# Other places in the issue order for one chunk's tokens, two weight pieces and the root steps of a fused mLSTM and Fourier kernel

## The chip, the cores and the metric

The kernel runs on one core of a Trainium2 chip. The metric is device time of one execution in microseconds, the median of several runs. The kernel before takes 398.78 us (three runs, 398.45 to 399.27).

A core has a matrix engine (TensorE, PE in the profile, with PEld for its weight loads), VectorE (DVE), ScalarE (ACT), GpSimd (POOL) and SyncE (SP), which here only issues DMA transfers. Each works off a queue of its own in order; semaphores hold an instruction until what it reads has been written and what it overwrites has been read.

## The reference

```python
batch, n_heads, seq, head_dim = (4, 8, 768, 40)
for t in range(S):                                   # mLSTM cell
    m_new = np.maximum(f_gate[:, :, t] + m, i_gate[:, :, t])
    f_stab = np.exp(f_gate[:, :, t] + m - m_new)
    i_stab = np.exp(i_gate[:, :, t] - m_new)
    m = m_new
    C = f_stab[:, :, None, None] * C + i_stab[:, :, None, None] * np.einsum('bhd,bhe->bhde', vt, kt)
    n = f_stab[:, :, None] * n + i_stab[:, :, None] * kt
    h_tilde = np.einsum('bhde,bhe->bhd', C, qt)
    denom = np.maximum(np.abs(np.einsum('bhd,bhd->bh', n, qt)[:, :, None]), 1.0)
    y[:, :, t] = h_tilde / denom / (1.0 + np.exp(-o_gate[:, :, t]))
x = y.transpose(0, 2, 1, 3).reshape(B, S, H * D)     # (4, 768, 320)
mixed = np.real(np.fft.fft(np.fft.fft(x, axis=1), axis=2))
u = x + mixed
un = (u - mean(u)) / np.sqrt(var(u) + 1e-06)         # over the last axis
out = u + np.maximum(un @ w_ch1, 0.0) @ w_ch2        # w_ch1 (320, 1280), w_ch2 (1280, 320)
```

## The kernel before

**Order by hand.** Every step is a function entered into a plan with `at(slot, phase, fn, ...)`; the plan is run in order of slot and then of phase (EVAC 0, FILL 1, MAIN 2, FILL_PE 3, with fractions between). Steps thus become instructions in that order, and each instruction goes to the queue of its engine. A step's place in the plan decides only what stands ahead of it on the engines that it uses.

**The mLSTM.** Tokens are processed in 6 chunks of 128 a batch, in a chunked form: scores of queries and keys, weighted by exponentials of gates (`mlstm_exp`, L548), a state C carried from chunk to chunk, and a division by the denominator. Batch 0 goes through `plan_mlstm`, three slots a chunk; the other batches go through `plan_halves`, in halves of 64 tokens, interleaved with the MLP of the batch before. For one chunk of batch 0: `mlstm_from_state` and `mlstm_from_chunk` make the heads (PE, `hb<-qg,C` and `hb<-W,kvt`), `mlstm_to_state` the chunk's part of the state (`pc`), `mlstm_add` (L643) adds it to C on VectorE, `mlstm_decay` (L586) scales C on GpSimd. `mlstm_heads` copies the heads out of PSUM (L630), `mlstm_turn` (L636) transposes them into `px`, a PSUM tile with a single buffer, and `mlstm_finish` (L759 to L766) reads `px`: denominator `den` (L759 to L761), output gate `so` (L763), then the product that writes the chunk's rows of `x` (L766).

**Rows at the wrong end.** For the Fourier step, chunks 3, 4 and 0 run backwards in time in a layout where one token of chunk 4 belongs into row 0 of chunk 3, and chunk 3's own row 0 into row 0 of chunk 4 (likewise chunks 1 and 0). `mlstm_rows` moves these: part 0 saves chunk 3's row (ScalarE, L773, `s_last`), part 1 copies chunk 4's row to chunk 3 (VectorE, L775), part 2 writes the saved row to chunk 4 (ScalarE, L777).

**The Fourier step.** `mix_fold` (L859 to L871) adds and subtracts chunks in pairs (0, 5), (1, 4), (2, 3), the last pair first, into `fe` (and `fe_odd` for the second pair); for batch 0 VectorE makes the sums, GpSimd the differences of the pairs (2, 3) and (1, 4). `mix_seq` (L937) multiplies by the sequence DFT (`pz`), `mix_feat` (L970) by the feature DFT (`pu`). `mix_add` (L984 to L998) adds the result to x chunk by chunk in the order 0, 5, 1, 4, 2, 3 and takes mean and variance; for chunk 4 it first copies one row of its own (L984, L985) that a product of `mix_feat` writes (`hb`). `mix_center` (L1006, ScalarE) subtracts the mean, `mix_turn` (L1017) transposes on TensorE and `mix_turn_out` (L1022, ScalarE) copies the result to `uT`.

**The root.** `mix_rstd` (L1030 to L1035, VectorE) makes a first guess of 1/sqrt(var), and three calls of `mix_rstd_step` (L1041 to L1044, four GpSimd instructions each) refine it. It is used when the MLP's output is scaled and stored (`mlp_store`, L1252).

**The MLP and its weights.** `mlp_in` (L1101, L1110) makes `pm` from `uT`, `mlp_relu` (L1126, ScalarE) the activation `h`, `mlp_out` (L1246) the output. The two weight matrices arrive as 64-bit floats, in ten pieces of 640 KB (five each), and every piece is turned into 32-bit floats on the chip: `load` (L452, a DMA into one of two `raw` buffers), `take` (L462, L464, VectorE: exponent and mantissa bits into `e` and `m`, one buffer each), `convert` (L469, L470, ScalarE) and `join` (VectorE, in three parts: L477 makes `e`, L480 `m`, L484 their product `w_sb`). Pieces are counted from 0 in the code, so the change's pieces 3 and 4 are `pieces[2]` and `pieces[3]`. The list `when` gives the plan's places of take, convert and join.

**Around the change.** VectorE's order from chunk 1's statistics (L998) on is: row copies and addition of chunk 4 (L984 to L998), joining `e` of piece 3, addition of chunk 2 and of chunk 3, joining `m` and `w_sb` of piece 3, taking piece 4. ScalarE's order at that place is: centring of chunks 4 and 2, eight exponentials of batch 1, conversion of piece 4, `uT`, `h`.

Of the kernel before, what the change touches and what calls it, by code (L numbers as in the profile page):

```python
# [10 lines left out]
FP = mybir.dt.float32  # L11
# [8 lines left out]
L = 128  # L20
# [37 lines left out]
def kernel(  # L58
# [379 lines left out]
    class Piece:  # L438
# [26 lines left out]

        def convert(self):
            if self.float:
                return
            nc.scalar.activation(out=self.e, in_=self.e, func=AF.Relu, scale=2.0**23, bias=ebias)  # L469
            nc.scalar.activation(out=self.m.bitcast(FP), in_=self.m, func=AF.Copy, scale=2.0**-20, bias=1.0)  # L470

# [274 lines left out]

    def mlstm_finish(b, c):

        k = chunks.pop((b, c))
        if c == 0:  # L750
            xs[b] = x_bufs[b % 2]
            nc.gpsimd.memset(xs[b][:, :, DM:DM + 1], 0.0)
        h1 = k.px.rearrange("p (a n) (i e) -> p a (n i) e", a=2, i=2) if b == 0 else k.ph
        den = tp.tile([L, H], FP, name="den", tag="den")

        def two(t):
# [7 lines left out]
                                       op0=OP.add, op1=OP.mult)  # L764
        x, sc = (t.rearrange("p (a h d) -> p a h d", a=2, d=D) for t in (xs[b][:, c, 0:DM], k.so))
        nc.vector.tensor_tensor(out=x, in0=h1[:, :, :, 0:D], in1=sc, op=OP.mult)  # L766

# [11 lines left out]
    def plan_mlstm(b):  # L779
        for c in range(NT):  # L780
# [18 lines left out]
            t, phase = ((6, 0.3), (9, -0.3), (12, -0.3), (15, -0.3), (16.5, 0.4), (18.5, 0))[c]  # L799
            at(t, FILL + phase, mlstm_finish, b, c)  # L800
        for c, part, t, phase in ((1, 0, 7, 0.3), (1, 1, 9, -0.2), (1, 2, 10, -0.1), (4, 0, 16, 0.01), (4, 1, 16.5, 0.45),
                                  (4, 2, 18, 0)):
            at(t, FILL + phase, mlstm_rows, b, c, part)

    def plan_halves(b, s0, stride=3):
        at(s0 - 2, FILL + 0.7, halves_start, b)
        for c in range(NT):
# [9 lines left out]
            at(s - 1, FILL, mlstm_scale_v, b, c)  # L817
            e = s - 1 if (b, c) != (1, 0) else s - 2
            at(e, FILL, mlstm_exp, b, c, 0)
            at(e, FILL + 0.5, mlstm_exp, b, c, NP)  # L820
            at(s, FILL, mlstm_mask, b, c)
# [224 lines left out]
    def plan_mix(b, s0, x_done, s_feat, s_add, s_turn):  # L1046
# [31 lines left out]
        for c, a, t in zip(ORDER, s_add, s_turn):  # L1078
            at(a, FILL if b < 2 else MAIN + 0.5, mix_add, b, c)
            at(*((a, FILL + 0.25) if b == 0 and c in (4, 2) else (t, FILL + 0.1)), mix_center, b, c)  # L1080
            at(t, FILL_PE + (5 if b == 0 or c in ORDER[:4] else -0.1), mix_turn, b, c)
            if b > 0:
                at(t, FILL_PE + 6, mix_turn_out, b, c)
            elif t < s_mlp:
                at(t + 1, FILL + 0.2, mix_turn_out, b, c)
            else:
                at(t + 1, EVAC, mix_turn_out, b, c)
# [291 lines left out]
    def plan_batch(b, s_mlstm, s_mix, s_mlp):  # L1379
# [21 lines left out]
        for n in range(3):  # L1401
            at(s + 3 * n if b == 0 else s, FILL + 0.65, mix_rstd_step, b)
        plan_mlp(b, s_mlp)
# [9 lines left out]

    when = [((2, 0.7), (4, 0.5), None), ((18.5, 0.7), (20, 0.7), (21, 0.6)), ((21.5, 0.7), (26, 0.7), None)]
    when += [((s, 0.7), (s + 1, 0.7), (s + 2, 0.6)) for s in (31, 33, 36, 39, 42, 48, 51)]
    pieces = w1_pieces + w2_pieces
    for n, (w, p) in enumerate(zip(when, pieces)):
        if n > 2:
            at(when[n - 2][2][0] + 1 if n != 4 else 31, FILL + 0.7, p.load)
        for t, fn in zip(w, (p.take, p.convert, p.join)):  # L1420
            if t:
                at(t[0], FILL + t[1], fn)
    for part, s in enumerate((7, 10, 13)):
        at(s, FILL - 0.35, pieces[0].join, part)
    for part in range(3):
        at(28 + part, FILL + 0.3, pieces[2].join, part)

# [161 lines left out]
```

## Time and profile before

| what | value |
| --- | --- |
| median of the runs | 398.78 us (398.45 to 399.27) |
| the profiled execution | 400.37 us, of which 398.5 us are its span |
| ScalarE, GpSimd: share of the span | 44%, 34% |
| DMA | 43.96 MB in 21614 packets, mean 110 GB/s |

All times within the trace are microseconds from the start of the span. A timeline row has start, duration, engine, line, operation, `out<-in` by the program's names, shapes and `x` the number of instructions in the row; in brackets at its end stands how long the engine idled ahead of it and which engine's instruction released it. Rows of like instructions are drawn together, and ends of matmuls are modelled, so rows of TensorE can overlap by some tenths.

### The profile page before, as it was taken

How to read it: one execution, taken by the hardware profiler on the slowest of the kernel's cores; microseconds unless marked ns; L12 is line 12 of the kernel's file. 1: busy time of each engine (PE TensorE's matmuls, PEld its weight loads, DVE VectorE, ACT ScalarE, POOL GpSimd, SP SyncE). 2: the span in 40 equal slices, each digit the busy share in tenths (PEclk: the TensorE clock that was granted, in tenths of full speed). 3: DMA queues.
4: the chain of work that ended last, by engine and by line, in shares of the span. 5: the costliest groups of instructions: out<-in, count | busy, mean ns of one | idle time of the engine just before them, and what ended most of it. 6: DMA issues, size and time to landing. Idle time of an engine off the chain costs nothing.

```text
span 398.5 us, 10881 instructions
## 1 busy us (share of the span) xinstructions
PE 383.7 (96%) x4342; PEld 278.1 (70%) x4342; DVE 280.7 (70%) x668; ACT 175.3 (44%) x505; POOL 134.1 (34%) x238
## 2 busy tenths in 40 slices
PE   8999897989999999999999998999999999999996
PEld 6887454545667677656469898766579997556996
DVE  8788859987699466779774688777854785336652
ACT  5978656675433233574442324563440023454000
POOL 5753325674855332363241314562300000020000
PEclk9999899899999999999999999999999999999999
DMA  7968496596983233455000713620000000000000
GB/s 223 305 182 317 107 238 194 159 251 198 258 207 91 89 100 128 137 176 165 2 1 9 231 62 113 194 67 3 0 2 16 19 33 35 0 0 2 34 35 33
DMA packets 21614, 43.96 MB, mean 110 GB/s; under 512 B 3492, under 2 KB 9852, under 8 KB 21436
## 3 DMA queue, kind: packets, MB, share of 16 engines
q1 hardware_dynamic: 21564, 43.27, 36.2%
q8 instruction: 34, 0.56, 0.6%
q14 instruction: 16, 0.13, 0.1%
HBM read 39.16 MB, written 4.10 MB: 109 GB/s over the span
## 4 chain that ended last, share of the span: by engine, by line
PE 78%; DVE 12%; issue 3%; POOL 1%; ACT 1%; DVEq 0%; POOLq 0%; ACTq 0%
PE po L1302 21%; PE pm L1173 16%; PE po L1246 8%; PE pm L1178 6%; PE ph L579 4%; PE pm L1110 4%; PE pu L970 3%; PE ps L579 3%; PE pz L925 2%; DVE so L763 2%; PE pm L1101 2%; PE put L1017 1%; PE hb L579 1%; PE pzt L925 1%; PE pz L937 1%
## 5 line engine op out<-in xcount | busy, mean ns | idle before, releaser
L1252 DVE SCALAR_TENSOR_TENSOR x<-po,rstd,x 128x160 f32<-128x160 f32 (+1 forms) x69 | 27.2, 394 | 39.4 <-PE po L1302 36.3
L1182 DVE TENSOR_TENSOR h<-h,pm 128x384 f32<-128x384 f32 x60 | 30.6, 549 | 26.7 <-PE pm L1178 12.4
L575 POOL TENSOR_SCALAR_AFFINE_SELECT W<-W 64x512 f32<-64x512 f32 x36 | 28.1, 781 | 36.2 <-ACT W L548 32.8
L1173 PE MATMUL pm<-uT,w_sb 128*128 128x384 f32 x90 | 37.8, 507 | 0.2 <-DVE uT L1161 0.2
L702 POOL TENSOR_TENSOR C<-C,decB 128x164 f32<-128x164 f32 x33 | 18.3, 555 | 57.1 <-DVE C L709 55.8
L548 ACT ACTIVATE W<-W,colT 128x64 f32<-128x64 f32 x144 | 36.5, 336 | 0.0
L1110 PE MATMUL pm<-uT,w_sb 128*128 128x384 f32 x80 | 30.6, 514 | 3.7 <-ACT h L1126 1.9
L1246 PE MATMUL po<-w_sb,h 128*128 128x320 f32 x120 | 34.1, 435 | 0.0
L560 POOL TENSOR_TENSOR qg<-qk,Gb 128x512 f32<-128x512 f32 x21 | 28.0, 1335 | 11.6 <-DMA qk<-in_qkT 11.3
L1041 POOL TENSOR_TENSOR t<-rstd 128x6 f32<-128x6 f32 x12 | 4.0, 334 | 81.7 <-DVE v L1035 81.2
L1302 PE MATMUL po<-T,S 128*128 128x160 f32 x180 | 28.0, 302 | 1.1 <-DVE x L1252 1.1
L1246 PEld LDWEIGHTS po<-w_sb,h 128*128 128x128 f32 x120 | 22.3, 190 | 9.2 <-issue 0.6
L1302 PEld LDWEIGHTS po<-T,S 128*128 128x128 f32 x180 | 25.4, 190 | 2.7 <-DVE x L1252 1.3
L1178 PE MATMUL pm<-uT,w_sb 64*128 64x384 f32 x120 | 26.6, 511 | 0.3 <-DVE h L1182 0.3
L1302 PE MATMUL po<-w_sb,h 128*128 128x160 f32 x180 | 26.3, 300 | 0.0
L1302 PEld LDWEIGHTS po<-w_sb,h 128*128 128x128 f32 x180 | 25.2, 190 | 1.5 <-DVE x L1252 0.3
L1173 PEld LDWEIGHTS pm<-uT,w_sb 128*128 128x128 f32 x90 | 15.4, 189 | 13.9 <-DVE h L1182 5.9
L1110 PEld LDWEIGHTS pm<-uT,w_sb 128*128 128x128 f32 x80 | 14.2, 194 | 15.0 <-issue 4.4
L1229 ACT ACTIVATE h<-h 128x384 f32<-128x384 f32 x45 | 23.1, 520 | 3.0 <-DVE h L1182 3.0
L1006 ACT ACTIVATE uc<-x 128x384 f32<-128x384 f32 x24 | 14.4, 614 | 20.7 <-DVE x L998 20.7
L709 DVE TENSOR_TENSOR C<-C,ps 128x164 f32<-128x164 f32 x33 | 10.5, 318 | 16.7 <-PE ps L579 10.0
L1178 PEld LDWEIGHTS pm<-uT,w_sb 64*128 64x128 f32 x120 | 12.9, 185 | 13.0 <-issue 8.2
(259 smaller groups left out, 848.6 us busy)
## 6 DMA issues: line engine op xcount, KB each, us to landing
kvt<-in_kv SPq DMA_DIRECT2D x24, 336.0 KB
qk<-in_qkT SPq DMA_DIRECT2D x48, 160.0 KB
raw<-in_w SPq DMA_DIRECT2D x10, 640.0 KB
Gb<-G_d SPq DMA_DIRECT2D x42, 128.0 KB
W<-M_d SPq DMA_DIRECT2D x36, 128.0 KB
so<-in_o SPq DMA_DIRECT2D x24, 160.0 KB
out<-x SPq DMA_DIRECT2D x24, 160.0 KB
ds_sb<-in_dft_s SPq DMA_DIRECT2D x1, 1158.0 KB
```

Source lines behind the costliest of these rows:

```text
L548: nc.scalar.activation(out=k.W[:, h, :], in_=M, func=AF.Exp, scale=-1.0, bias=colT[:, c, 0, b * H + h:b * H + h + 1])
L560: nc.gpsimd.tensor_tensor(out=k.qg[:, :, t], in0=k.qk[:, 0, :, t], in1=k.Gb[:, :, t], op=OP.mult)
L575: nc.gpsimd.affine_select(out=W, in_=W, compare_op=OP.is_ge, fill=0.0, base=base, pattern=[[0, H], [-1 if back else 1, LH]], channel_multi ...
L579: nc.tensor.matmul(out, w, x, start=start, stop=True, skip_group_check=True)
L1110: nc.tensor.matmul(k.pm[i], w1_block(ch, f // 2 * 2 + i), u[2 * ch], start=(ch == 0 and not ahead), stop=(ch == 1 and ahead), skip_group_c ...
L1173: nc.tensor.matmul(bank, w, u, start=start, stop=True, skip_group_check=True)
L1178: nc.tensor.matmul(bank, w1_rest(i)[rows], mlp_u(gr, 1)[rows], start=False, stop=True, skip_group_check=True)
L1182: nc.vector.tensor_tensor(out=h, in0=h, in1=bank, op=OP.add)
L1229: nc.scalar.activation(out=h, in_=h, func=AF.Relu, scale=-1.0)
L1246: nc.tensor.matmul(k.po[m], hidden(gr, f)[:, i * L:(i + 1) * L], w2_sb[:, f, :], start=(f == 0), stop=(f == NFF - 1))
L1252: nc.vector.scalar_tensor_tensor(out=u, in0=po, scalar=k.rstd[:, c:c + 1], in1=u, op0=OP.mult, op1=OP.add)
L1302: nc.tensor.matmul(po, a[:, f], w[:, f], start=start and f == 0, stop=f == half - 1, skip_group_check=True)
```

## The change

It moves and splits steps; nothing else is computed.

- `mlstm_add` of chunks 1, 2 and 3 stood behind a third of the joining of weight piece 1 (FILL - 0.35); that third now comes at FILL - 0.28, behind the add.
- `mlstm_finish` of chunk 4 has two parts. Part 0 makes `den` and `so` and then the product for one row, which is written directly to row 0 of chunk 3; the copy of that row (`mlstm_rows` part 1) is left out. Part 1 makes the product for all 128 rows; it stands behind the fold of pair (2, 3) and ahead of the fold of pair (1, 4).
- Weight piece 3: its conversion and the joining of `e` come before chunk 0's addition to x; `m` and `w_sb` are joined between chunk 1's statistics and chunk 4's row copies. Piece 4: its taking follows there, its conversion goes in two halves between the centrings of chunks 4 and 2, and its joining stands behind chunk 3's statistics. Its raw load, and that of piece 5, move ahead on SP: the order of issues there was so, raw, so, Gb, Gb, raw and is raw, so, raw, so, Gb, Gb.
- The eight exponentials of batch 1's first chunk are issued as two lots of four with the conversion of piece 4 and a centring between. The centring of chunk 3 moves ahead of one copy of `uT`.
- The root steps of batch 0 go from slots 43, 46 and 49 to 48, 49 and 50. On GpSimd the first now stands behind the last state decay of batch 1 and ahead of the fold into `fe_odd`, the other two behind that fold and ahead of batch 2's first `qg`.

TensorE's order is the same in both kernels.

```diff
-        def convert(self):
+        def convert(self, part=None):
             if self.float:
                 return
-            nc.scalar.activation(out=self.e, in_=self.e, func=AF.Relu, scale=2.0**23, bias=ebias)
-            nc.scalar.activation(out=self.m.bitcast(FP), in_=self.m, func=AF.Copy, scale=2.0**-20, bias=1.0)
+            if part != 1:
+                nc.scalar.activation(out=self.e, in_=self.e, func=AF.Relu, scale=2.0**23, bias=ebias)
+            if part != 0:
+                nc.scalar.activation(out=self.m.bitcast(FP), in_=self.m, func=AF.Copy, scale=2.0**-20, bias=1.0)
...
-    def mlstm_finish(b, c):
-
-        k = chunks.pop((b, c))
+    def mlstm_finish(b, c, part=None):
+
+        k = chunks.pop((b, c)) if part != 0 else chunks[b, c]
...
+        def tokens(rows, to):
+            x, sc = (t.rearrange("p (a h d) -> p a h d", a=2, d=D) for t in (xs[b][rows, to, 0:DM], k.so[rows]))
+            nc.vector.tensor_tensor(out=x, in0=h1[rows, :, :, 0:D], in1=sc, op=OP.mult)
+
+        if part == 1:
+            return tokens(slice(0, L), c)
...
-        x, sc = (t.rearrange("p (a h d) -> p a h d", a=2, d=D) for t in (xs[b][:, c, 0:DM], k.so))
-        nc.vector.tensor_tensor(out=x, in0=h1[:, :, :, 0:D], in1=sc, op=OP.mult)
+        tokens(*((slice(0, 1), c - 1) if part == 0 else (slice(0, L), c)))
...
-            at(t, FILL + phase, mlstm_finish, b, c)
-        for c, part, t, phase in ((1, 0, 7, 0.3), (1, 1, 9, -0.2), (1, 2, 10, -0.1), (4, 0, 16, 0.01), (4, 1, 16.5, 0.45),
+            if c == 4:
+                at(t, FILL + phase, mlstm_finish, b, c, 0)
+                at(17, FILL + 0.15, mlstm_finish, b, c, 1)
+            else:
+                at(t, FILL + phase, mlstm_finish, b, c)
+        for c, part, t, phase in ((1, 0, 7, 0.3), (1, 1, 9, -0.2), (1, 2, 10, -0.1), (4, 0, 16, 0.01),
                                   (4, 2, 18, 0)):
...
-            e = s - 1 if (b, c) != (1, 0) else s - 2
-            at(e, FILL, mlstm_exp, b, c, 0)
-            at(e, FILL + 0.5, mlstm_exp, b, c, NP)
+            early = (b, c) == (1, 0)
+            at(*((27, FILL + 0.22) if early else (s - 1, FILL)), mlstm_exp, b, c, 0)
+            at(*((28, FILL + 0.3) if early else (s - 1, FILL + 0.5)), mlstm_exp, b, c, NP)
...
-            at(*((a, FILL + 0.25) if b == 0 and c in (4, 2) else (t, FILL + 0.1)), mix_center, b, c)
+            at(*(((32, EVAC + 0.1) if c == 3 else (a, FILL + 0.25) if c in (4, 2) else (t, FILL + 0.1)) if b == 0 else
+                 (t, FILL + 0.1)), mix_center, b, c)
...
-            at(s + 3 * n if b == 0 else s, FILL + 0.65, mix_rstd_step, b)
+            at(48 + n if b == 0 else s, FILL + 0.65, mix_rstd_step, b)
...
-    when = [((2, 0.7), (4, 0.5), None), ((18.5, 0.7), (20, 0.7), (21, 0.6)), ((21.5, 0.7), (26, 0.7), None)]
-    when += [((s, 0.7), (s + 1, 0.7), (s + 2, 0.6)) for s in (31, 33, 36, 39, 42, 48, 51)]
+    when = [((2, 0.7), (4, 0.5), None), ((18.5, 0.7), (20, 0.7), (21, 0.6)), ((21.5, 0.7), (23, 0.15), None)]
+    when += [((26, 0.7), None, (29, 0.5)), ((30, 0.7), (34, 0.7), (35, 0.6))]
+    when += [((s, 0.7), (s + 1, 0.7), (s + 2, 0.6)) for s in (36, 39, 42, 48, 51)]
...
-            at(when[n - 2][2][0] + 1 if n != 4 else 31, FILL + 0.7, p.load)
+            at(when[n - 2][2][0] + 1 if n != 4 else 27, FILL + 0.7, p.load)
...
-        at(s, FILL - 0.35, pieces[0].join, part)
-    for part in range(3):
-        at(28 + part, FILL + 0.3, pieces[2].join, part)
+        at(s, FILL - 0.28, pieces[0].join, part)
+    for part, (s, phase) in enumerate(((24, -0.1), (26, 0.3), (26, 0.32))):
+        at(s, FILL + phase, pieces[2].join, part)
+    for part in range(2):
+        at(27, FILL + (0.23, 0.3)[part], pieces[3].convert, part)
```

## The prediction

> **What bounds the kernel now.** I read the page first: its span and the busy shares.
>
> ```profile
> span 398.5 us, 10881 instructions
> PE 383.7 (96%) x4342; PEld 278.1 (70%) x4342; DVE 280.7 (70%) x668; ACT 175.3 (44%) x505; POOL 134.1 (34%) x238
> ```
>
> TensorE is busy for 96% of the span. Only two things can be won back: the 14.8 us in which it stands, and time in which its clock is halved. The profiled execution took 400.37 us, 1.87 us more than its span and 1.59 us more than the median 398.78 of the runs shown; all terms below are taken from its trace, and their sum is applied to the median. The change lies between 30 and 116 us, so the second view was TensorE's waits there, grouped by releaser (total us, times, longest); these lead the list, three shorter ones come below with their own rows.
>
> ```profile
> PE pm L1110 <- ACT h L1126: 1.9, 1, 1.9
> PE pm L1110 <- issue: 1.6, 1, 1.6
> ```
>
> The third view was busy time and granted clock in stretches (TensorE, its weight loads, VectorE, ScalarE, GpSimd; then clock, DMA share, GB/s).
>
> ```profile
> 39.00:42.40 3.40, 2.31 (x17) 1.54 (x16) 3.16 (x7) 2.67 (x10) 2.00 (x3) 1.00 0.15 44
> 42.40:45.80 3.40, 3.40 (x9) 1.13 (x8) 3.12 (x9) 2.28 (x10) 1.88 (x4) 0.51 0.69 193
> 66.30:69.70 3.40, 1.59 (x6) 0.88 (x7) 3.05 (x5) 2.73 (x7) 2.96 (x5) 1.00 0.65 228
> 69.70:73.10 3.40, 3.40 (x8) 1.30 (x7) 3.33 (x5) 3.11 (x11) 2.28 (x4) 0.51 0.49 137
> 83.30:86.80 3.50, 2.17 (x81) 1.37 (x73) 3.29 (x8) 3.00 (x11) 2.44 (x3) 1.00 0.91 267
> ```
>
> The clock was halved twice, each time for 3.4 us right after a stretch in which TensorE stood much (busy 2.31 and 1.59 of 3.40); 2.17 of 3.50 at 83 us did not halve it. A halved stretch does 3.40 x 0.51 = 1.7 us of full-clock work, so it costs about 1.7 us. The two starts are 27.3 us apart, eight times 3.41: the decision seems to fall on a grid.
>
> **The change part by part.**
>
> *1. State add before the weight join.* In chunks 1 to 3 of batch 0, VectorE now adds the state C (L643) before it joins a third of weight piece 1 (L477, L480 or L484). In the last of these:
>
> ```profile
> 31.95 1.24 DVE L484 TENSOR_TENSOR w_sb<-m,e 128x640 f32<-128x640 f32 x1
> 32.24 0.61 PE L636 MATMUL px<-ident,h 128*128 128x128 f32 x4
> 33.12 0.31 DVE L643 TENSOR_TENSOR C<-C,pc 128x164 f32<-128x164 f32 x1
> 33.57 0.67 PE L579 MATMUL hb<-qg,C 40*64 40x128 f32 x16 [0.72 <-DVE den L759]
> ```
>
> The add waited behind the 1.24 us join, and TensorE's next product stood 0.72 us for it. Ahead of the join it is done before TensorE's transposes end at 32.24 + 0.61 = 32.85, so the product starts 0.72 us earlier. The wait list has no other entry of that kind, so for the two earlier joins, which TensorE's own work covers, I take nothing.
>
> *2. Fifth chunk's tokens in two parts.* The finish of chunk 4 multiplied all 128 rows (L766) and then copied the one row that belongs to chunk 3 (L775). Now it writes that one row first, straight to its place; the fold of the third pair (eo, fe) follows, then the product of all rows, then the fold of the second pair.
>
> ```profile
> 39.33 0.49 DVE L766 TENSOR_TENSOR x<-px,so 128x320 f32<-128x320 f32 x1
> 39.92 0.32 DVE L775 COPY x<-x 1x320 f32<-1x320 f32 x1
> 39.97 0.63 PE L636 MATMUL px<-ident,h 128*128 128x128 f32 x4
> 40.27 0.49 DVE L859 TENSOR_TENSOR eo<-x 128x321 f32<-128x321 f32 x1
> 40.80 0.76 DVE L863 TENSOR_TENSOR fe<-eo 128x161 f32<-128x161 f32 x1
> 41.62 2.16 PE L937 MATMUL pz<-ds_sb,fe 128*128 128x386 f32 x4 [1.02 <-DVE fe L863]
> ```
>
> Before, from 39.33, product, copy, eo and fe ended at 41.56 and released pz at 41.62. With the 0.72 us of step 1, the new order starts at 38.61. A product of one row with two inputs isn't in the trace: it costs between the one-row copy's 0.32 and the full product's 0.49, and I take 0.49, as the length is set by the elements in a row (320 in both). Then eo 0.49, fe 0.76: fe ends about 40.45. But px has one buffer: the transposes of chunk 5 at 39.97 need the full product to have read it, and they stand ahead of pz in TensorE's order. The product, 0.49 us after fe, ends at about 41.0; transposes 0.63 more, so pz starts at about 41.6, as before. The wait on fe becomes a wait on the product, one engine step earlier, and the 0.72 us won is lost again. Bounds: 0.7 us gain if the row takes 0.32 and fe 0.33 (as the next one in the trace did), 0.7 us loss if step 1 yields no lead. I take 0. The product also delays the second pair's fold (row copy L777 waits for it), which is read only after pz's 2.16 us. The stretch 39.0 to 42.4 keeps its idle time, so the first halving stays.
>
> *3. Weight pieces 3 and 4 and the first exponentials.* Here the largest stop lies. VectorE's part of piece 3 (L480, L484) and the taking of piece 4 (L462, L464) stood behind chunk 3's statistics; they now go ahead of a copy (L984) that waits for a product.
>
> ```profile
> 56.07 0.18 DVE L998 BATCH_NORM_AGGREGATE x<-stats 128x2 f32<-128x6 f32 x1
> 58.31 0.32 DVE L984 COPY pu<-hb 1x160 f32<-1x160 f32 x1 [2.06 <-PE hb L970]
> 60.07 0.18 DVE L998 BATCH_NORM_AGGREGATE x<-stats 128x2 f32<-128x6 f32 x1
> 61.14 0.49 PE L1017 MATMUL ph<-ident,uc 128*128 128x128 f32 x3
> 63.14 0.79 DVE L480 SCALAR_TENSOR_TENSOR m<-raw,m 128x640 f32<-128x640 uint32 x1
> 63.97 0.83 DVE L484 TENSOR_TENSOR w_sb<-m,e 128x640 f32<-128x640 f32 x1
> 64.83 0.84 DVE L462 TENSOR_SCALAR e<-raw 128x640 uint32<-128x640 uint32 x1
> 65.59 0.94 DVE L464 TENSOR_SCALAR m<-raw 128x640 uint32<-128x640 uint32 x1
> ```
>
> VectorE idles 2.06 us ahead of 58.31. The four cost 0.79 + 0.83 + 0.84 + 0.94 = 3.4 us by these rows; the taking of the piece before was shorter and one join later longer:
>
> ```profile
> 50.12 0.49 DVE L462 TENSOR_SCALAR e<-raw 128x640 uint32<-128x640 uint32 x1
> 82.68 1.28 DVE L480 SCALAR_TENSOR_TENSOR m<-raw,m 128x640 f32<-128x640 uint32 x1
> ```
>
> With 0.49 for each half of a taking it is 2.6 us; with 1.28 for the first it is 3.9. From 56.25, 2.6 to 3.9 us puts L984 at 58.85 to 60.15; I take 59.2, the lower price with 0.35 us for gaps between four instructions, as the row of the taking nearest in time is the short one. That is 0.9 us late. Chunk 4's statistics (60.07 before) and its turn on TensorE (L1017, 61.14 before, with no wait of TensorE's own) move by the same 0.9: the turn starts near 62.0, after a new wait of 0.9 us. The 1.9 us stop comes later:
>
> ```profile
> 65.70 0.83 ACT L469 ACTIVATE e<-e,ebias 128x640 uint32<-128x640 uint32 x1 [1.34 <-DVE e L462]
> 66.56 0.74 ACT L470 ACTIVATE m<-m 128x640 f32<-128x640 uint32 x1
> 67.56 0.88 ACT L1126 ACTIVATE h<-pm 128x384 f32<-128x384 f32 x2
> 68.11 0.91 PE L1110 MATMUL pm<-uT,w_sb 128*128 128x384 f32 x2 [1.86 <-ACT h L1126]
> ```
>
> ScalarE's two conversions of the next piece (1.57 us) stood ahead of uT and the activation h that TensorE waited for from 66.25 to 68.11. They now go between 60 and 62.7 among the exponentials, which are cut in two lots of four. Without them h could start at 67.56 - 1.57 = 66.0 and have the first of its two instructions (0.44) done by 66.4, whereas TensorE's 5.1 us of work between chunk 4's turn (61.14) and the stop (66.25) now ends at 62.0 + 5.1 = 67.1. So the matmul of 68.11 starts at 67.1 without waiting: the stop of 1.9 us goes and the wait of 0.9 us comes, 1.0 us won. Bounds: 1.9 if L984 isn't late at all (58.85 with a cover of its own), 0.1 if it starts at 60.15. The moved DMA issues (weights' raw load ahead of gates and decays) have slack on SP: the decays Gb issued at 64.87 slip by some 2 us, and their reader comes late:
>
> ```profile
> 64.87 1.80 SPq L535 DMA_DIRECT2D Gb<-G_d  x2
> 77.15 1.27 POOL L560 TENSOR_TENSOR qg<-qk,Gb 128x512 f32<-128x512 f32 x1
> ```
>
> *4. The second halving.* With the stop gone, the stretch 66.3 to 69.7 has TensorE busy for nearly all its 3.4 us, so by the rows above it shouldn't be followed by a halved stretch: 1.7 us won. [...]
>
> *5. Root steps later.* GpSimd's first step of the reciprocal root stood ahead of a mask:
>
> ```profile
> 98.89 0.78 POOL L1041 TENSOR_TENSOR t<-rstd 128x6 f32<-128x6 f32 x1 [1.56 <-DVE v L1035]
> 101.54 1.38 POOL L575 TENSOR_SCALAR_AFFINE_SELECT W<-W 64x512 f32<-64x512 f32 x2
> 106.52 0.68 PE L579 MATMUL ph<-C,qg 40*64 40x41 f32 x32 [0.53 <-DVE x L766]
> ```
>
> The mask begins 2.6 us earlier without it, VectorE's work behind it moves up by as much, the last of it the product of tokens for which TensorE waited 0.53 us, and that wait goes: 0.5 us won. The steps now lie around the odd row's fold and ahead of the next batch's qg, after which GpSimd idles 2.21 us before its next mask, and the result is needed only when this batch's output is scaled (L1252):
>
> ```profile
> 123.39 2.23 POOL L575 TENSOR_SCALAR_AFFINE_SELECT W<-W 64x512 f32<-64x512 f32 x2 [2.21 <-DMA so<-in_o]
> ```
>
> Without that cover the 2.5 us would fall on the next batch's first mask. One stop is left:
>
> ```profile
> 87.10 1.88 PE L1110 MATMUL pm<-uT,w_sb 128*128 128x384 f32 x5 [1.63 <-issue]
> ```
>
> It stands in the middle of like matmuls, waits on nothing the change touches, and stays.
>
> Sum: 0 - 1.0 - 1.7 - 0.5 = -3.2 us, and 398.78 - 3.2 = **395.6 us**; the profiled execution would take about 400.37 - 3.2 = 397.2.
>
> **The rivals.**
>
> *B, the clock still halves.* The new 0.9 us wait at chunk 4's turn lies in 59.5 to 62.9 or, with the grid elsewhere, in one stretch with what is left of the stop. For it: 2.31 of 3.40 busy did halve the clock. Against it: 2.17 of 3.50 did not. Only term 4 falls: 395.6 + 1.7 = 397.3 us.
>
> *C, VectorE jams ahead of L984.* If the four take 3.9 us and the copies and statistics behind L984 (58.31 to 60.07) are drawn out as well, chunk 4's turn moves to about 63, TensorE stands 2 us there instead of at h, and terms 3 and 4 fall. Left is 0.5: 398.3 us, no change. For it: the same taking (L462) took 0.49 and 0.84 us, the same join (L480) 0.79 and 1.28. [...] Against it: the taking and the join nearest in time have the short rows.
>
> *D, slower.* The same jam, when L984 starts after 60.6 us: TensorE's wait at the turn, over 2.2 us and across 62.9, then leaves both stretches beside it part idle, as 2.31 of 3.40 us at 39 was, and two are followed by a halved one instead of one: 398.3 + 1.7 = 400.0 us. For it: 1.28, 1.28, 0.84 and 0.94, the longest rows of each kind, make 4.3 us, which is just that. Against it: all four would have to be long.
>
> *E, the issue stop moves.* If the 1.63 us stop depends on where the instruction stream then stands, it may vanish (395.6 - 1.6 = 394.0) or appear twice (397.2). Against it: nothing near it changes.
>
> **How the numbers follow.** Forecast 0.46, B 0.22, C 0.10, D 0.12, E 0.10. A change under 0.2% (0.8 us) can't be told from none here. Faster: forecast, B and E, 0.78; same: C, 0.10; slower: D, 0.12. Range: down to 393.7, which takes in E's 394.0 and the bounds of parts 2 and 3 together (0.7 + 0.9 below the forecast: 394.0) with 0.3 for the scatter of the runs; up to 398.9, which takes in C and leaves out D. The likeliest's own range is 394.0 to 397.0.
>
> **What would show it.** Right: the product after chunk 3's add starts about 0.7 us earlier at 33; chunk 5's transposes wait on VectorE's x and pz begins at about 41.6; a wait on uc of some 0.9 us at chunk 4's turn; no stop on h; full clock from 66 to 73; no wait on x at 106. Wrong: L984 after 60.2, a halved stretch after 60 us, or pz past 42.3.

## The result, and the profile after

The changed kernel takes 394.43 us (four runs, 394.26 to 394.97) against 399.02 us for the kernel before: a ratio of 0.9889, 95% interval 0.9871 to 0.9906. The forecast was 395.6. Five slow runs of the groups below, over 1.5% above the fastest run of their kernel there (four of the kernel before, one of e12), are left out of the numbers there. The top of the page of the changed kernel, with its queue of instruction transfers:

```profile
span 392.9 us, 10881 instructions
PE 379.7 (97%) x4342; PEld 277.5 (71%) x4342; DVE 281.2 (72%) x668; ACT 174.6 (44%) x505; POOL 134.9 (34%) x238
...
q8 instruction: 34, 0.56, 0.6%
```

TensorE is busy 4.0 us less and stands 13.2 us instead of 14.8. Its waits between 30 and 114 us, with the same columns as before:

```profile
PE px L638 <- DVE x L758: 1.6, 1, 1.6
PE ph L1028 <- ACT uc L1017: 1.4, 1, 1.4
PE put L1028 <- ACT uc L1017: 1.2, 1, 1.2
PE pm L1122 <- issue: 0.7, 1, 0.7
```

Of the waits on h, fe and den and of the one on x at 106 us none is left, and the one without a releaser (`issue`) is less than half as long. Two are new, that of chunk 5's transposes on the product (x, at 41 us) and that at chunk 4's turn, and the one on uc at chunk 0's turn has grown. In the trace of before that one was:

```profile
PE put L1017 <- ACT uc L1006: 0.3, 1, 0.3
```

The same stretches as before up to 73 us, with the granted clock third from the end, and one more, around the new wait at chunk 4's turn:

```profile
39.00:42.40 3.40, 1.82 (x14) 1.28 (x13) 2.72 (x6) 1.63 (x6) 2.16 (x3) 1.00 0.37 135
42.40:45.80 3.40, 3.40 (x15) 1.51 (x15) 3.12 (x9) 3.20 (x14) 1.81 (x4) 1.00 0.25 61
59.50:62.90 3.40, 2.04 (x10) 0.88 (x10) 3.18 (x9) 1.93 (x5) 0.00 (x0) 1.00 0.92 227
66.30:69.70 3.40, 3.40 (x15) 1.73 (x15) 2.25 (x5) 2.39 (x10) 2.69 (x5) 1.00 0.97 312
69.70:73.10 3.40, 3.40 (x134) 2.54 (x133) 2.40 (x3) 2.71 (x7) 3.24 (x5) 1.00 0.67 182
```

The clock is full in all of them, also behind the stretches in which TensorE was busy for 1.82 and 2.04 of 3.40 us. Both halvings are gone in this execution.

The timeline around the parts (1 and 2):

```profile
32.46 0.31 DVE L645 TENSOR_TENSOR C<-C,pc 128x164 f32<-128x164 f32 x1
32.69 1.00 DVE L486 TENSOR_TENSOR w_sb<-m,e 128x640 f32<-128x640 f32 x1
33.10 0.67 PE L581 MATMUL hb<-qg,C 40*64 40x128 f32 x16
...
38.93 0.48 DVE L758 TENSOR_TENSOR x<-px,so 1x320 f32<-1x320 f32 x1
39.97 0.76 DVE L874 TENSOR_TENSOR fe<-eo 128x161 f32<-128x161 f32 x1
40.65 0.48 DVE L758 TENSOR_TENSOR x<-px,so 128x320 f32<-128x320 f32 x1
41.28 0.63 PE L638 MATMUL px<-ident,h 128*128 128x128 f32 x4 [1.58 <-DVE x L758]
41.74 1.46 PE L948 MATMUL pz<-ds_sb,fe 128*128 128x386 f32 x4
```

The state add is ahead of the join and the product behind it no longer waits for VectorE. (The row of before named `den`, L759, as what ended that wait. Here the product starts at 33.10 us and den at 33.62, so it was the add that held it.) The one-row product takes 0.48 us, as a full one. The transposes of chunk 5 wait 1.58 us for the full product, and pz starts at 41.74. Then the two new waits on uc, and what is ahead of them on VectorE:

```profile
51.44 0.82 DVE L479 SCALAR_TENSOR_TENSOR e<-raw,e 128x640 uint32<-128x640 uint32 x1 [0.49 <-ACT e L470]
54.11 0.55 PE L1028 MATMUL put<-ident,uc 128*128 128x128 f32 x3 [1.17 <-ACT uc L1017]
...
55.57 1.09 DVE L482 SCALAR_TENSOR_TENSOR m<-raw,m 128x640 f32<-128x640 uint32 x1
56.70 0.97 DVE L486 TENSOR_TENSOR w_sb<-m,e 128x640 f32<-128x640 f32 x1
57.70 0.91 DVE L462 TENSOR_SCALAR e<-raw 128x640 uint32<-128x640 uint32 x1
58.53 0.48 DVE L464 TENSOR_SCALAR m<-raw 128x640 uint32<-128x640 uint32 x1
58.93 0.31 DVE L995 COPY pu<-hb 1x160 f32<-1x160 f32 x1
61.63 0.55 PE L1028 MATMUL ph<-ident,uc 128*128 128x128 f32 x3 [1.36 <-ACT uc L1017]
65.64 0.88 ACT L1138 ACTIVATE h<-pm 128x384 f32<-128x384 f32 x2
```

The join of `e` (L479) stands ahead of chunk 0's addition, and TensorE waits 1.17 us at that chunk's turn (0.35 before). The four weight instructions fill the time to 58.93, 1.3 us after the row's product would have allowed the copies, and chunk 4's turn waits 1.36 us. The activation h is ready before TensorE asks for it.

Executions differ at their start, since TensorE's clock rises at different times. The first change of the clock that the trace records, to full, is at 4.9 us in before and at 10.8 us in e1 (below); the same eight matmuls (L232, the second such group) took 1.05 us in the one and 1.92 in the other, and the first product with a carried state, `hb<-qg,C`, starts at 18.87 and 21.25 us (18.75 to 21.25 in all traces). So starts of the same TensorE instructions are compared from that one on, each the row's start less the start of that product; "(h)" marks executions with a halved stretch ahead of the row:

```
us after first hb<-qg,C   before   after  e1      e2     e12    e3      e5
fourth hb<-qg,C            14.70   13.79  14.69   13.79  14.69  13.78   13.78
pz of the third pair       22.75   22.43  23.33   21.83  22.73  22.42   22.83h
turn of chunk 0            35.84h  34.80  36.37h  34.38  35.28  33.97   36.69h
turn of chunk 4            42.27h  42.32  43.55h  42.21  42.84  40.40   43.35h
turn of chunk 3            50.13h  47.69  48.92h  47.58  48.20  48.52h  48.72h
ph<-C,qg, first            55.83h  51.74  52.96h  51.63  52.25  53.80h  52.76h
ph<-C,qg, third            73.66h  68.57  69.89h  69.22  71.31  70.64h  69.77h
ph<-C,qg, fifth            87.65h  81.95  83.27h  82.61  84.70  84.02h  83.75h
```

(e1, e2, e12, e3 and e5 are the changed kernel with parts undone, below.) Up to chunk 4's turn the changed kernel has won nothing on the profiled execution of before, although a halved stretch is gone: 42.32 against 42.27. Then it wins 2.5 us to chunk 3's turn (the stop on h), 1.6 more to the first `ph<-C,qg` (the second halved stretch), 1.0 to the third (the stop without a releaser), 0.6 to the fifth (the root steps): 5.7 us. The medians differ by 4.4 to 4.6 us; the profiled execution of before was 1.35 us above the later median of 399.02, for a reason that comes out below.

### The profile page after: what moved, and what is told of

Read it like the earlier page. It is cut to its first block, busy times and chain, and to the rows that moved or that the text cites. A ratio compares the mean times of both kernels' runs of the same rounds, so it can differ in the third digit from the quotient of the medians.

```text
span 392.9 us, 10881 instructions
## 1 busy us (share of the span) xinstructions
PE 379.7 (97%) x4342; PEld 277.5 (71%) x4342; DVE 281.2 (72%) x668; ACT 174.6 (44%) x505; POOL 134.9 (34%) x238
## 4 chain that ended last, share of the span: by engine, by line
PE 80%; DVE 11%; ACT 2%; issue 2%; DVEq 0%; ACTq 0%
PE po L1314 21%; PE pm L1185 16%; PE po L1258 8%; PE pm L1122 7%; PE pm L1190 6%; PE ph L581 5%; PE ps L581 4%; PE pu L981 3%; PE pz L936 2%; PE pm L1113 2%; PE hb L581 1%; PE put L1028 1%; PE pzt L936 1%; DVE so L771 1%; PE ps L598 1%
## 5 line engine op out<-in xcount | busy, mean ns | idle before, releaser
L704 POOL TENSOR_TENSOR C<-C,decB 128x164 f32<-128x164 f32 x33 | 19.1, 578 | 58.6 <-DVE C L711 52.5
L1185 PE MATMUL pm<-uT,w_sb 128*128 128x384 f32 x90 | 37.8, 507 | 0.2 <-DVE uT L1173 0.2
L1122 PE MATMUL pm<-uT,w_sb 128*128 128x384 f32 x80 | 29.3, 499 | 0.7 <-issue 0.7
L1033 ACT COPY uT<-put 128x384 f32<-128x384 f32 x21 | 9.6, 477 | 26.9 <-PE put L1028 26.8
```

What stands on the lines that cost most here:

```text
L1122: nc.tensor.matmul(k.pm[i], w1_block(ch, f // 2 * 2 + i), u[2 * ch], start=(ch == 0 and not ahead), stop=(ch == 1 and ahead), skip_group_c ...
L1185: nc.tensor.matmul(bank, w, u, start=start, stop=True, skip_group_check=True)
```

## The experiments

In each group the kernel before ran beside the others; its medians were 398.73, 398.87, 399.32 and 398.68 us. All edits are made to the changed kernel.

**The changed kernel again.** No edit.

> The changed kernel itself once more, beside the others of this group. If the grid on which the clock is halved lies differently from run to run, its runs scatter by up to 2 us as those of the kernel before did (396.4 to 400.8) and its median is above the first 394.4 us, 394.5 to 395.5; its trace may show a halved stretch at 39 to 46 us although the first had none. If the change itself removed the halving, all runs lie at 394.3 to 395.0 us with full clock.

Measured: 395.18 us (five runs, 394.51 to 396.30), ratio 0.9924, interval 0.9894 to 0.9954. That is 0.75 us more than the first time; the median of all nine runs of the changed kernel is 394.75 us. The scatter goes in part with the clock, of which each run has its mean. Of the nine runs of the changed kernel six had 0.998 or more, with a median of 394.5 us; two had 0.995 and 0.996 (395.7 and 395.0) and one 0.991 (396.3). Of 79 runs of the kernel before:

```
mean granted clock     runs   median us   lowest to highest
0.998 to 1.0            35     397.8       396.4 to 399.6
0.994 to 0.996          18     399.0       398.4 to 401.0
0.990, 0.991            26     399.8       399.1 to 403.1
```

A halved stretch of 3.4 us at half clock lowers the mean over 397 us by 0.0043, so the second row has one such stretch and the third two (of the traces, e1 has 0.996 with one, e5 and b1 have 0.991 with two); where they lie the mean does not say. The kernel before thus had none of "its" two halvings in 35 of 79 runs, and two halved stretches in 26; its profiled execution was one of those. One costs 1.2 us, two 2.0. At full clock the kernels stand at 397.8 and 394.5 us, 3.3 us apart. Runs of one row still lie up to 4 us apart. One cause is the start: the views read a clock of 1.00 there even where the matmuls took 1.92 us instead of 1.05, so its differences of up to 2.5 us are not in the mean clock, and only a trace shows them.

**Part 1 undone.**

```diff
-        at(s, FILL - 0.28, pieces[0].join, part)
+        at(s, FILL - 0.35, pieces[0].join, part)
```

> The changed kernel with part 1 undone (state add behind the weight join again). The prediction's accounting: the 0.7 us lead is missing, so the product that follows chunk 3's add waits about 0.7 us again, chunk 4's token product and chunk 5's transposes start 0.7 us later, and nothing between them makes it good: 394.4 + 0.7 = 395.1 us. Rival, the lead is lost anyway (the wait on px sets the end of the stage by something else): 394.4 us. Second rival: 0.7 us more idle time ahead of pz halves the clock there again: 395.1 + 1.7 = 396.8 us, with a halved stretch near 43 us.

Measured: 396.32 us (ten runs, 395.76 to 397.87). In the table the fourth `hb<-qg,C` is 0.90 us late (0.77 of it in the last of the three joins, the rest in the one before), and pz still 0.90: nothing made it good. In this trace the clock was halved behind pz:

```profile
41.40:44.80 3.40, 1.56 (x13) 1.27 (x14) 2.65 (x6) 1.32 (x4) 1.74 (x3) 1.00 0.18 57
44.80:48.20 3.40, 3.40 (x8) 0.96 (x6) 3.09 (x9) 3.37 (x16) 2.23 (x4) 0.51 0.21 43
```

and eight of the ten runs had a mean clock of 0.995 or 0.996. So the halved stretch of the second rival came in most runs (where, only the trace shows), and it cost little: 1.6 us of halving at the second pair's pz is 0.3 us at chunk 4's turn, since the waits on uc there swallow it. The two runs at full clock took 395.94 and 396.66 us, no less than the others. Their distance to 394.5 us is twice the 0.9 us of the table; what else is in it stays open.

**Part 2 undone.**

```diff
-            if c == 4:
-                at(t, FILL + phase, mlstm_finish, b, c, 0)
-                at(17, FILL + 0.15, mlstm_finish, b, c, 1)
-            else:
-                at(t, FILL + phase, mlstm_finish, b, c)
+            at(t, FILL + phase, mlstm_finish, b, c)
...
-                                  (4, 2, 18, 0)):
+                                  (4, 1, 16.5, 0.45), (4, 2, 18, 0)):
```

> The changed kernel with part 2 undone (full product, row copy, fold). The prediction's accounting says the split loses the 0.7 us that part 1 wins, since chunk 5's transposes wait for the late full product. So without the split pz starts about 0.7 to 0.8 us earlier (near 41.0) and the kernel takes 393.6 us, if the clock near 43 us stays full. Rival, the split is what took the first halved stretch away: a halved stretch near 42 to 46 us is back, 394.4 - 0.8 + 1.4 = 395.0 us or more.

Measured: 395.55 us (ten runs, 394.10 to 399.63), all ten at full clock; the rival with the halved stretch falls. pz is 0.60 us earlier without the split, as expected, but chunk 4's turn only 0.11: the wait on uc took the rest (1.7 us there instead of 1.4). The time is no better; in this trace the stop without a releaser is longer and takes what was left:

```profile
PE ph L1024 <- ACT uc L1013: 1.7, 1, 1.7
PE pm L1118 <- issue: 1.4, 1, 1.4
```

**Parts 1 and 2 undone together.** Both edits above.

> The changed kernel with parts 1 and 2 undone together, so parts 3 and 5 alone. By the prediction, what part 1 wins is lost again in part 2: the same time as the changed kernel, 394.4 us in the control's terms (difference 0). By the traces with one part undone, part 1 is worth 0.9 us at pz and part 2 loses 0.6 us of it there, of which 0.1 is left at chunk 4's turn: the pair is worth 0.5 to 0.8 us, so 0.5 to 0.8 us slower than the control. Rival, the issue stop at 84 us is 0.7 us longer without the split (1.6 and 1.4 us in the two traces without it, 0.7 to 0.9 with it): 1.2 to 1.5 us slower than the control.

Measured: 396.96 us (nine runs, 395.40 to 397.49), ratio 0.9925, interval 0.9888 to 0.9963. At chunk 4's turn the pair is worth 0.52 us (42.84 against 42.32), the second expectation's lower end; the rest is that stop again, 2.9 us here:

```profile
PE pm L1118 <- issue: 2.9, 1, 2.9
PE ph L1024 <- ACT uc L1013: 1.4, 1, 1.4
...
PE hb L581 <- DVE den L767: 0.7, 1, 0.7
```

**Part 3 undone.**

```diff
-    when = [..., ((21.5, 0.7), (23, 0.15), None)]
-    when += [((26, 0.7), None, (29, 0.5)), ((30, 0.7), (34, 0.7), (35, 0.6))]
+    when = [..., ((21.5, 0.7), (26, 0.7), None)]
+    when += [((s, 0.7), (s + 1, 0.7), (s + 2, 0.6)) for s in (31, 33)]
...
-    for part, (s, phase) in enumerate(((24, -0.1), (26, 0.3), (26, 0.32))):
-        at(s, FILL + phase, pieces[2].join, part)
-    for part in range(2):
-        at(27, FILL + (0.23, 0.3)[part], pieces[3].convert, part)
+    for part in range(3):
+        at(28 + part, FILL + 0.3, pieces[2].join, part)
```

(also the load of piece 5, the exponentials and chunk 3's centring as before)

> The changed kernel with part 3 undone (pieces 3 and 4, exponentials, chunk 3's centring at their old places). The prediction's accounting: the wait on h of 1.9 us and one halved stretch near 70 us are back, the new waits at the turns (0.8 us at 54 and 1.2 us at 61 more than before) go: +1.9 + 1.7 - 2.0 = +1.6, 396.0 us. By the prediction as it stood (1.0 + 1.7) 397.1 us. Rival, the first halved stretch and half of the issue stop at 87 us also hang on part 3: 396.0 + 1.4 + 0.9 = 398.3 us, little under the kernel before.

Measured: 397.00 us (eight runs, 396.04 to 397.64), 1.8 to 2.6 us slower than the changed kernel. The stop on h is back, and a halved stretch behind it:

```profile
PE pm L1122 <- ACT h L1138: 1.9, 1, 1.9
...
63.60:67.00 3.40, 1.53 (x5) 0.68 (x4) 3.05 (x5) 2.67 (x6) 2.81 (x5) 1.00 0.96 320
67.00:70.40 3.40, 3.40 (x9) 1.66 (x9) 3.33 (x4) 2.20 (x9) 2.57 (x3) 0.51 0.27 40
```

Without part 3 chunk 4's turn is 1.9 us earlier (40.40 against 42.32), and the stop on h of 1.9 us gives that back: the waits by themselves are worth next to nothing. What is left at the first `ph<-C,qg`, 2.06 us, is the halved stretch (1.7) and 0.4. By their mean clocks five of the eight runs had a halved stretch. But the three without one took 396.04, 396.24 and 397.64 us, 1.5 to 3.1 us above the changed kernel's 394.5 at full clock, and the 0.4 us of this one trace does not account for them. None of the three has a trace, so what costs them this time stays open.

**Part 5 undone.**

```diff
-            at(48 + n if b == 0 else s, FILL + 0.65, mix_rstd_step, b)
+            at(s + 3 * n if b == 0 else s, FILL + 0.65, mix_rstd_step, b)
```

> The changed kernel with part 5 undone (root steps ahead of the mask again). The prediction's accounting: TensorE's wait of 0.5 to 0.6 us on the token product near 101 us is back, 395.0 us. Rival, GpSimd has so much lead in the changed kernel that the wait doesn't come back: 394.4 us.

Measured: 395.72 us (six runs, 394.89 to 397.70). The wait is back, 0.5 us, and from the third to the fifth `ph<-C,qg` the table gives 13.98 us against 13.38: 0.6 us. The accounting holds (the four runs at full clock have a median of 395.3 us, 0.7 above 394.5). The rest of this trace's time is the clock, which was halved for two stretches on end around pz, where this part changes nothing:

```profile
PE ph L581 <- DVE x L758: 0.5, 1, 0.5
...
41.40:44.80 3.40, 2.88 (x8) 1.92 (x8) 2.65 (x8) 2.90 (x13) 2.58 (x5) 0.50 0.06 15
44.80:48.20 3.40, 3.40 (x10) 1.51 (x9) 2.76 (x7) 2.29 (x9) 0.20 (x1) 0.53 0.75 205
```

**Less weight work ahead of the copies.** Three tries to take the two new waits away. The first:

```diff
-    when += [((26, 0.7), None, (29, 0.5)), ((30, 0.7), (34, 0.7), (35, 0.6))]
+    when += [((30, 0.7), (33, 0.3), (34, 0.5)), ((34, 0.7), (35, 0.7), (36, 0.6))]
...
-    for part, (s, phase) in enumerate(((24, -0.1), (26, 0.3), (26, 0.32))):
+    for part, (s, phase) in enumerate(((26, 0.3), (26, 0.32), (29, 0.3))):
```

(and the two halves of piece 4's conversion no longer at slot 27)

> The changed kernel, but VectorE has only the two short-path joins of piece 3 (e, m) in the idle time ahead of chunk 4's row copies; w_sb of piece 3 and the taking of piece 4 come behind chunk 3's addition, and ScalarE's conversions of piece 4 behind the activation h. If the two new waits on uc (1.2 us at chunk 0's turn, 1.4 at chunk 4's) come from the join ahead of chunk 0's addition and from the jam ahead of the copies, they fall to 0.3 and 0.2 us, chunk 4's turn starts 1.7 to 2.0 us earlier and, with no stop on h, the kernel is 1.5 to 1.9 us faster than the control. Rival, the late conversions make a new wait on piece 4's or 5's weights or on the masks of the next chunk: no faster than the control, with a wait on ScalarE's W or h between 66 and 80 us.

Measured: 398.29 us (396.10 to 400.43), no better than the kernel before. The first half of the expectation held: waits on uc of 0.4 and 0.6 us, and the first `ph<-C,qg` 1.6 us earlier than in the changed kernel (50.14 against 51.74 after the first product). The rival took more back:

```profile
PE ps L581 <- DVE C L711: 1.8, 1, 1.8
...
PE ph L581 <- ACT warm L747: 0.8, 1, 0.8
```

With part 2 undone as well:

> As the run before, and with part 2 undone as well. If the split costs 0.4 us at chunk 0's turn, which the wait on uc no longer swallows, 0.4 us faster than the run before; rival, the issue stop at 84 us is 0.7 us longer without the split: 0.3 us slower than the run before.

Measured: 395.79 us (six runs, 394.98 to 396.59), with the same new waits (1.5 and 0.8 us): better than the try before, by more than its 0.4 us, and no better than the changed kernel. Why by so much stays open; the clock was halved for one stretch in this run's trace, and for two, from 82.3 us on, in that of the try before.

The second try moves less:

```diff
-    when += [((26, 0.7), None, (29, 0.5)), ((30, 0.7), (34, 0.7), (35, 0.6))]
+    when += [((27, 0.12), None, (29, 0.5)), ((30, 0.7), (34, 0.7), (35, 0.6))]
...
-    for part, (s, phase) in enumerate(((24, -0.1), (26, 0.3), (26, 0.32))):
+    for part, (s, phase) in enumerate(((26, 0.3), (26, 0.32), (27, 0.1))):
...
-        at(27, FILL + (0.23, 0.3)[part], pieces[3].convert, part)
+        at(27, FILL + (0.26, 0.3)[part], pieces[3].convert, part)
```

> The changed kernel with only e and m of piece 3 joined in the idle time ahead of chunk 4's row copies, and w_sb of piece 3 and the taking of piece 4 between chunk 4's and chunk 2's additions; everything later as in the changed kernel. If the waits on uc (1.2 us at chunk 0's turn, 1.4 to 1.6 at chunk 4's) come from VectorE's order there, both fall below 0.5 us and TensorE reaches the turn of chunk 4 about 2.0 us earlier; without the late conversions of the run before last the lead should stay to 72 us at least: 1.0 to 2.0 us faster than the changed kernel (two medians, 394.4 and 395.2), 393.0 to 394.0 us. Rival, VectorE's work behind (additions of chunks 2 and 3, then the state adds) sets the pace and TensorE waits there instead: 394.5 to 395 us, with a wait on uc, on VectorE's C or on ACT's h between 62 and 80 us.

Measured: 396.54 us (394.74 to 399.50). Chunk 4's turn comes 1.67 us earlier, but chunk 2's turn then waits 1.0 us for a copy of uT that stands behind ScalarE's exponentials, and the stop without a releaser is 2.3 us:

```profile
PE pm L1122 <- issue: 2.3, 1, 2.3
...
PE ph L1028 <- ACT uT L1033: 1.0, 1, 1.0
PE ph L1028 <- ACT uc L1017: 0.5, 1, 0.5
PE put L1028 <- ACT uc L1017: 0.4, 1, 0.4
```

Behind that stop the clock was halved for one stretch, from 85.7 us on. VectorE's rows of this run show how far a price can move: the join of `m`, 0.81 to 1.36 us elsewhere in it, takes 1.89 just here.

```profile
57.32 1.89 DVE L482 SCALAR_TENSOR_TENSOR m<-raw,m 128x640 f32<-128x640 uint32 x1
```

The third try is the second with the second lot of exponentials behind that copy:

```diff
-            at(*((28, FILL + 0.3) if early else (s - 1, FILL + 0.5)), mlstm_exp, b, c, NP)
+            at(*((32, EVAC + 0.05) if early else (s - 1, FILL + 0.5)), mlstm_exp, b, c, NP)
```

> The run with two joins ahead of the copies, and the second lot of four exponentials behind the copy of uT for which chunk 2's turn waited 1.0 us there. If that lot was what delayed the copy, the wait of 1.0 us at chunk 2's turn is gone or under 0.2 us, and TensorE keeps 1.4 to 1.7 us of lead on the changed kernel (start differences taken off) up to 72 us. On the whole time: if the stop without a releaser near 84 us stays at 0.7 us, 393.0 to 393.8 us; rival, the stop lengthens again as in the three other variants with a lead here (1.1 and 2.3 us, or in its place waits on VectorE's C and ScalarE's warm), and the time is 395 to 397 us, no better than the changed kernel.

Measured: 396.30 us (394.27 to 399.22). The wait on uT is gone; a wait of 0.4 us on h and one of 1.3 us on GpSimd's `vw` come instead, and the stop is 1.0 us:

```profile
PE ps L581 <- POOL vw L568: 1.3, 1, 1.3
PE pm L1122 <- issue: 1.0, 1, 1.0
```

TensorE's lead was 1.6 us up to chunk 2's turn and 0.9 at the first `ph<-C,qg`, and behind the wait on `vw` the clock was halved for one stretch, from 73.1 us on; the rival held. No try beats the changed kernel.

**The stop without a releaser.** It stands at the same TensorE instruction, the fourth of a group of like matmuls, in every trace where nothing else stops TensorE just before: 1.6 us before, 0.7 after (and 0.7 again), 0.8, 1.4, 2.9, 0.7 and 0.9 us in e1, e2, e12, e3 and e5. The instruction queue moved 34 packets with 0.56 MB, 16 KB each; TensorE executes 4342 matmuls and as many weight loads, so if these are its instructions, a packet holds, as an estimate, 8684 / 34 = some 255 of them. In narrow windows of the DMA view one such packet arrives at 79.7 us in the trace after, and TensorE goes on at 82.55; with 2.9 us of stop at 82.6 and 85.18; in before at 84.4 and 87.10. The stop ends 2.5 to 3.2 us after the packet in all eight of these traces, and 2.4 to 2.8 after it in four later ones (b3, b4 and the two runs below). The packet does not come at a fixed place of TensorE's work: it follows the start of the second `ph<-C,qg` by 1.5 us after, 2.5 before and 3.9 in e12, and the longer that is, the longer the stop (0.7, 1.6, 2.9 us). Whether data under way ahead of it decides when it comes:

```diff
+    when[6] = ((40, 0.7), (41, 0.7), (42, 0.6))
...
-            at(when[n - 2][2][0] + 1 if n != 4 else 27, FILL + 0.7, p.load)
+            at({4: 27, 6: 38}.get(n) or when[n - 2][2][0] + 1, FILL + 0.7, p.load)
```

> The changed kernel with the load of piece 7 (640 KB, issued at 76.1 us) and its taking, conversion and joining one to two slots later, so that less data is under way ahead of the 16 KB instruction packet that arrives at 79.7 us, 2.8 us before TensorE's stop without a releaser ends at 82.55. If the packet stands behind that data, it arrives before 78.5 us and the stop of 0.7 us goes: 0.5 to 0.7 us faster than the changed kernel. Rival, the packet is asked for late by the engine itself and not delayed by data: the stop stays at 0.7 us, no change.

Measured: 399.38 us (397.56 to 402.11), no better than the kernel before. The packet came at 80.4 us, not before 78.5, and the stop is 1.1 us: that load is not what holds it. The later taking also made TensorE wait 1.6 us for VectorE's C:

```profile
PE ps L581 <- DVE C L711: 1.6, 1, 1.6
...
PE pm L1122 <- issue: 1.1, 1, 1.1
```

Together with the second try:

> The two runs before together. If both do what is expected of them: 392.5 to 393.5 us. If TensorE's 2 us of lead only brings it earlier to the place where instructions are missing, the stop there grows by what was won, and the time stays at 394 to 395 us.

Measured: 397.89 us (396.81 to 399.66), slower than either expectation, with both sets of waits (stop 1.1, uT 1.0, `vw` 0.9, `warm` and C 0.7 us each). What sets the time of the packet stays open.

## Why the prediction was right, and where it was not

**The time** fell in the range and 1.2 us from the forecast (395.6 against 394.43; 0.9 with the median of all nine runs). That it came so near is in part luck: by the accounts below the terms of part 3 and of the halving were too large by 0.6 and 1.2 us, and gains of 0.5 us (parts 1 and 2), 0.9 us (the stop without a releaser) and about as much that is not traced were not in the sum.

**Part 1** was mis-sized a little: 0.7 us were forecast, 0.9 measured, as the join before the last one also delayed its chunk (0.13 us), which had been put at nothing.

**Part 2** held as a mechanism: the wait on fe became one on the product, pz came at 41.74 (forecast 41.6; with the later start of this execution taken off it is 0.3 us earlier than before), the one-row product cost 0.48 (0.49). Its price is 0.60 us at pz, not the whole 0.72. That the pair nets to 0 was wrong by 0.52 us in the changed kernel's favour, shown with both undone. "The first halving stays" failed: neither it nor its absence belongs to the kernel. TensorE stood more around pz than before (busy 1.82 of 3.40 us), and the clock was full; in e5 the same work ran for two stretches at half clock, and in i1, with the same idle time, for one.

**Part 3** had the right stop and the right cure: h's wait went to nothing. The term of -1.0 us was mis-sized. Forecast was one new wait of 0.9 us; measured are 1.4 us at chunk 4's turn (the four instructions cost 1.09, 0.97, 0.91 and 0.48, 3.45 us in place of the 2.95 taken; the long rows of L462 and L480 quoted for the bound came nearer) and 1.2 us at chunk 0's turn, 0.8 more than before. That second wait was overlooked: `e` joined ahead of chunk 0's addition was not costed at all. With part 3 undone these two waits go and the stop returns, and the difference in that trace is 0.4 us, not 1.0. The three runs of e3 at full clock, 1.5 to 3.1 us slower, speak for more, so the size of this term at full clock stays open. Rival D's "longest rows of each kind" were not the longest: the trace of before has 1.24 us for L484 and 1.03 for L462 and for L464, with L480's 1.28 4.6 us in place of 4.3.

**Term 4**, the second halving, was right in direction, and in its cause as far as e3's trace shows it: with the stop back, a halved stretch follows it. It was wrong in kind: it was taken as certain, and it happens in some of the runs. The kernel before has at least one halved stretch in 44 of 79 runs and two in 26, at 1.2 and 2.0 us: 18 x 1.2 and 26 x 2.0 over 79 are 0.9 us on average. The mean of the changed kernel's nine runs, less their full-clock median, gives 0.4. So some 0.5 us of the gain is the clock's, against 1.7 in the sum. The profiled execution of before was one of those with two, 1.35 us above the median, which the sum didn't allow for.

**Part 5** was right: 0.5 forecast, 0.6 measured, and no wait of TensorE behind the steps' new places is put down to them.

**The missing term** is the stop without a releaser, said to stay as nothing near it changes. It went from 1.6 to 0.7 us, 0.9 us of the gain in the traces, a good half of what rival E allowed. The runs without part 2 have 1.4 to 2.9 us there, those with it at the same places of the weight work 0.7 to 0.9; why an order of VectorE's instructions 40 us earlier should matter isn't shown.

Added up from the traces, without halvings: parts 1 and 2 0.5, part 3 0.4, part 5 0.6, the stop 0.9: 2.4 of the 3.3 us between 397.8 and 394.5. The remaining 0.9 us was not traced to a place; starts that differ and a larger part 3 are both possible. The runs at full clock with a part undone do not add up to the whole either: e12 (five runs, 397.0 us), e3 (three, 396.2) and e5 (four, 395.3) are 2.4, 1.7 and 0.7 us above 394.5, 4.8 us in sum where the kernels are 3.3 apart. So the prices depend on one another; the stop without a releaser, 2.9 us in e12 against 0.7, is one way in which they do.

## What to carry to other kernels

A wait that stands in one profile may be a matter of that execution: where the traces show a halved clock, look at the mean clock of every run before a halved stretch is put into a sum, and weigh it by how often it is there. When work is moved into an engine's idle time, cost it with the longest rows of its kind in the trace, and ask of every moved instruction what it now stands ahead of: the one small join that was not costed here made a longer new wait (0.8 us) than the error in the four that were (0.5 us). And a lead won ahead of a point where the next resource is late is not won: three tries gained 1.6 us at chunk 4's turn and were 2.3 to 3.6 us behind the changed kernel at the third `ph<-C,qg`, through new waits and, as said, one or two halved stretches behind them (1.7 us each).

## What the runs showed of the hardware

In the trace of before the clock changes on a grid: its recorded changes are to full at 4.90 us and to half at 42.45 and 69.76 us, for 3.41 us each, and their starts are 11 and 8 times 3.41 us apart. In e1 the clock rises at 10.8 us (the 16 matmuls `ps<-qk` from 9.42 us on, in which it rises, took 1.78 us, against 1.16 in before) and is halved from 44.9 us on, 10 times 3.41 us later. So the grid lies differently in the two executions. Where the work stands at the start differs too (the first product with a carried state is between 18.75 and 21.25 us). Whether a stop of 1 to 2 us is followed by a halved stretch differs as well: in before that of 1.02 us ahead of pz was, in the changed kernel that of 1.58 us ahead of the transposes was not. Ten times in these traces, their ends aside, the clock was halved for one or two stretches. Cut on the grid of its own execution, the stretch ahead had TensorE busy for 1.18 (b3) to 2.59 us (e5) of 3.41. But the time that TensorE is busy in such a stretch does not decide it: 2.33 us was followed by a halved clock (before, the first two lines) and 1.69 us was not (e12, the last two).

```profile
39.04:42.45 3.41, 2.33 (x15) 1.55 (x16) 3.17 (x7) 2.71 (x11) 2.05 (x3) 1.00 0.12 36
42.45:45.86 3.41, 3.41 (x9) 1.14 (x8) 3.13 (x9) 2.23 (x10) 1.83 (x4) 0.50 0.70 194
80.63:84.04 3.41, 1.69 (x41) 0.89 (x31) 3.20 (x8) 2.52 (x10) 2.42 (x4) 1.00 0.90 243
84.04:87.46 3.42, 2.28 (x9) 1.21 (x11) 3.39 (x7) 1.57 (x2) 3.27 (x4) 1.00 0.85 218
```

What decides it stays open. Runs of one kernel differ in it: the mean clocks of the 79 runs of the kernel before go from 0.990 to 1.0, with none, one or two halved stretches by the table of mean clocks.

TensorE stops inside a group of like matmuls, for 0.7 to 2.9 us depending on the kernel, and goes on 2.4 to 3.2 us after a 16 KB packet of the instruction queue in all twelve traces that have this stop. That it waits for that packet is inferred from this agreement.
